# Spreading a transform stage over the opening of a training-step kernel, folding its edges in with the rest, and moving small sums off two borders

## The chip, the cores and the metric

The kernel runs on one core of a Trainium2 chip. The metric is the device time of that core in microseconds (us). The kernel before took 1378.1 us, the median of three runs from 1374.69 to 1380.41.

## The reference, cut to what matters

The program computes a layer forward and, from `grad_out`, all its gradients. Sequence length S is 2048, width D is 1024, hidden width F is 3584, all tensors are bf16.

```python
g = sigmoid((x * gate_w).sum(-1, keepdims=True))
a = irfft2(rfft2(x) * (w_r + 1j * w_i))            # a filter over the whole S x D plane
h = relu(x @ w1 + b1) ** 2
b = h @ w2 + b2
out = g * a + (1 - g) * b
# outputs: out, and the gradients of x, w_r, w_i, w1, b1, w2, b2, gate_w
```

Two of the small outputs are sums over columns: the gradient of `b2` (`out_7` in the kernel) and that of `gate_w` (`out_8`). The gradient of `b1` is `out_5`.

## The kernel before

The kernel has four stretches in time:

- the opening (to about 97 us): transposes of x and of the gradient, the gate, the first pair of hidden blocks, and the first stage of the two-dimensional transform for the 16 tiles of x;
- pass 1 (to about 480 us): the products `ph` = x·w1 and `pd` = gradient·w2ᵀ for each hidden block, with the first transform stage of the gradient's 16 tiles mixed in;
- pass 2: the gradients of the weights (`pw`), with the middle and the last transform stages mixed in;
- the last products (`acc`, `accg`), which give `out` and the gradient of x.

One tile of the first stage goes through five steps. VectorE (DVE) folds the tile by sums and differences, TensorE (PE) does eight small products into `pk`, ScalarE (ACT) copies them to `ft`, PE does eight more into `pu`, ACT copies them to `u`, and a store issued from GpSimd (POOL) sends `u` to memory.

```python
def folds(fb, xt, earlier=None):
    uv = fb.tile([P, 2, H], FDT, name="uv", tag="uv", bufs=2)
    after(V(out=uv[:, 0, :], in0=xt[:, 0:H], in1=xt[:, H:D], op=ALU.add), earlier, mybir.DependencyClass.NoSync)
    V(out=uv[:, 1, :], in0=xt[:, 0:H], in1=xt[:, H:D], op=ALU.subtract)
    ...
    V(out=f[:, 4, 0:1], in0=uv[:, 0, 0:1], in1=uv[:, 0, Q : Q + 1], op=ALU.add)
    V(out=f[:, 4, P : P + 1], in0=uv[:, 0, 0:1], in1=uv[:, 0, Q : Q + 1], op=ALU.subtract)

def one_s1(fb, cf, T, i, f, kmat, earlier=None):
    ...                                            # pk, then ft by ACT
    pu = fps.tile([P, 2, H], FP32, name="pu", tag="ps2", bufs=2)
    column_stage(FWD, pu, ft, cf)                  # reads ft at once
    u = fb.tile([P, D], FDT, name="u", tag="u", bufs=2)
    ...                                            # u by ACT, then st(out=z_scr..., in_=u)
```

`after(ins, earlier, NoSync)` only fixes an order: in the compiled program `ins` stands behind `earlier`. `st` issues a transfer from POOL, `ld` one from SyncE (SP). In the driver the x tiles come in bunches of four; the gradient's follow at a quarter of a step for each step of the main work, from -1.5:

```python
for i0 in range(0, NT, 4):
    ...                                            # gate, turns, transposes, next(units)
    for i in range(i0, i0 + 4):
        one_s1(f1, cf, 0, i, folds(f1, xs[i]), kf[:])
first = first_stage_of_grad()
mixed = spread(units, first, 0.25, -1.5)
```

`move()` loads the turned w2 blocks (`w2T`) of the next group from memory by SP, and `group()` loads the first operand of pass 2 (`grp`) by SP as well.

## Time and profile before

| | before |
|---|---|
| span of the profiled execution | 1374.2 us |
| PE busy | 1339.7 us (97%) |
| end of the opening (80 to 94 us) | PE 10.27 of 14 us, clock 0.87 |
| end of the last PE instruction to the end of the span | 7.9 us |

PE bounds the kernel, so every gain must come out of the 34.5 us in which PE is idle, out of time at a lowered clock, or out of the end. The lines for this are in the prediction below.

### The profile page before, as it was taken

How to read it: one execution, taken by the hardware profiler on the slowest of the kernel's cores; microseconds unless marked ns; L12 is line 12 of the kernel's file. 1: busy time of each engine (PE TensorE's matmuls, PEld its weight loads, DVE VectorE, ACT ScalarE, POOL GpSimd, SP SyncE). 2: the span in 40 equal slices, each digit the busy share in tenths (PEclk: the TensorE clock that was granted, in tenths of full speed). 3: DMA queues.
4: the chain of work that ended last, by engine and by line, in shares of the span. 5: the costliest groups of instructions: out<-in, count | busy, mean ns of one | idle time of the engine just before them, and what ended most of it. 6: DMA issues, size and time to landing. Idle time of an engine off the chain costs nothing.

```text
span 1374.2 us, 18936 instructions
## 1 busy us (share of the span) xinstructions
PE 1339.7 (97%) x7146; PEld 643.0 (47%) x7146; DVE 750.9 (55%) x1541; ACT 409.7 (30%) x626; POOL 291.3 (21%) x469
## 2 busy tenths in 40 slices
PE   7989999999999999999999999999999999999997
PEld 5644444444444444444444444555545444444443
DVE  6966666666665575564445643323856575642222
ACT  6753344444443312222323223433212100000000
POOL 0222222322232233433432212212001000000000
PEclk9999999999999999999999999999999999999999
DMA  7547777787779778789677458766898664653430
GB/s 272 188 169 210 250 230 237 240 250 240 218 240 266 222 234 191 206 211 216 184 184 196 99 151 245 234 228 206 249 230 231 177 199 130 200 159 103 135 100 23
DMA packets 217029, 273.32 MB, mean 199 GB/s; under 512 B 16988, under 2 KB 152170, under 8 KB 216938
## 3 DMA queue, kind: packets, MB, share of 16 engines
q1 hardware_dynamic: 181162, 153.58, 41.8%
q0 software_dynamic: 35776, 118.54, 26.7%
q8 instruction: 56, 0.92, 0.3%
q14 instruction: 35, 0.29, 0.1%
HBM read 147.25 MB, written 118.51 MB: 193 GB/s over the span
## 4 chain that ended last, share of the span: by engine, by line
PE 50%; issue 37%; POOL 4%; DMA 2%; DVE 2%; ACT 1%; SPq 1%; POOLq 0%; DVEq 0%; ACTq 0%
PE pw L783 14%; PE pd L593 12%; PE ph L583 11%; PE pw L800 7%; PE pu L278 1%; DMA w1g<-in_B_w_dram 1%; POOL ax_scr L490 1%; POOL out_dram L809 1%; POOL out_dram L914 1%; POOL out_dram L873 1%; PE pk L251 1%; PE pv L363 1%; DMA z_scr<-u 1%; PE px L318 1%; PE px L317 1%
## 5 line engine op out<-in xcount | busy, mean ns | idle before, releaser
L583 PE MATMUL ph<-xT,w1g 128*128 128x512 bf16 x896 | 221.2, 384 | 1.2 <-ACT rT L585 1.2
L593 PE MATMUL pd<-dbT,w2T 128*128 128x512 bf16 x896 | 212.6, 380 | 5.2 <-issue 1.8
L800 PE MATMUL pw<-grd,res 128*128 128x512 bf16 x896 | 200.2, 379 | 0.0
L783 PE MATMUL pw<-dbn,grp 128*128 128x512 bf16 x896 | 198.0, 379 | 1.6 <-DVE row L735 1.6
L866 PE MATMUL acc<-w,hblk 128*128 128x512 bf16 x896 | 198.1, 379 | 1.2 <-DVE bGo L868 1.2
L907 PE MATMUL accg<-w1Tr,hblk 128*128 128x512 bf16 x896 | 193.6, 379 | 0.0
L593 PEld LDWEIGHTS <-w2T 128*128 128x128 bf16 x896 | 87.3, 98 | 110.5 <-issue 6.2
L907 PEld LDWEIGHTS <-hblk 128*128 128x128 bf16 x896 | 87.7, 98 | 105.7
L783 PEld LDWEIGHTS <-grp 128*128 128x128 bf16 x896 | 87.0, 98 | 105.9 <-issue 2.5
L583 PEld LDWEIGHTS <-w1g 128*128 128x128 bf16 x896 | 87.3, 99 | 100.8 <-issue 6.7
L866 PEld LDWEIGHTS <-hblk 128*128 128x128 bf16 x896 | 87.0, 98 | 100.8 <-issue 1.5
L800 PEld LDWEIGHTS <-res 128*128 128x128 bf16 x896 | 86.6, 98 | 98.8
L585 ACT ACTIVATE rT<-ph,b1col 128x512 bf16<-128x512 f32 x112 | 77.2, 689 | 180.4 <-PE ph L583 180.3
L597 DVE SCALAR_TENSOR_TENSOR dhT<-pd,rT 128x512 bf16<-128x512 f32 x112 | 75.4, 673 | 82.4 <-PE pd L593 65.9
L787 ACT CAST wo<-pw 128x512 bf16<-128x512 f32 x56 | 32.8, 586 | 164.9 <-PE pw L783 158.9
L912 DVE TENSOR_TENSOR gxo<-accg,g 128x512 bf16<-128x512 f32 x32 | 22.1, 691 | 107.4 <-PE accg L907 107.2
L698 DVE STREAM_TRANSPOSE stg<-h2T 128x512 int32<-128x512 int32 x56 | 39.6, 708 | 71.7 <-ACT h2T L586 71.7
L319 DVE CAST x<-px 128x1024 f16<-128x1024 f32 x16 | 19.6, 1225 | 107.2 <-PE px L318 107.2
L795 POOL DMA_DIRECT2D out_dram<-wo x112 | 56.2, 515 | 84.1 <-ACT wo L787 78.3
L805 ACT CAST wo<-pw 128x512 bf16<-128x512 f32 x56 | 32.9, 587 | 132.0 <-PE pw L800 125.7
L586 ACT ACTIVATE h2T<-rT 128x512 bf16<-128x512 bf16 x112 | 70.8, 632 | 3.0
L705 DVE STREAM_TRANSPOSE stgd<-dhT 128x1024 bf16<-128x1024 bf16 x56 | 68.7, 1228 | 0.7
(177 smaller groups left out, 1431.2 us busy)
## 6 DMA issues: line engine op xcount, KB each, us to landing
h2T_scr<-h2T POOLq DMA_DIRECT2D x28, 512.0 KB, 5.3
h_scr<-stg POOLq DMA_DIRECT2D x28, 512.0 KB, 6.9
dhT_scr<-dhT POOLq DMA_DIRECT2D x28, 512.0 KB, 7.1
dh_scr<-stgd POOLq DMA_DIRECT2D x28, 512.0 KB, 6.8
grp<-h_scr SPq DMA_DIRECT2D x112, 128.0 KB
grd<-dh_scr SPq DMA_DIRECT2D x112, 128.0 KB
hblk<-h2T_scr SPq DMA_DIRECT2D x8, 1792.0 KB
hblk<-dhT_scr SPq DMA_DIRECT2D x8, 1792.0 KB
```

Source lines behind the costliest of these rows:

```text
L583: mm(ph[:], lhsT=w1g[:, dc, fc % 2 * P : (fc % 2 + 1) * P], rhs=xT[:, dc, ss], start=(dc == 0), stop=(dc == DC - 1))
L585: nc.scalar.activation(rT[:], ph[:], ACT.Relu, bias=b1col[:, fc : fc + 1])
L586: nc.scalar.activation(h2T, rT[:], ACT.Square)
L593: mm(pd[:], lhsT=w_[:, ec // 2, ec % 2 :: 2], rhs=dbT[:, ec, ss], start=(ec == 0), stop=(ec == DC - 1),)
L597: return STT(out=dhT, in0=pd[:], scalar=2.0, in1=rT[:], op0=ALU.mult, op1=ALU.mult, accum_out=gb1part[:, fc, sb : sb + 1],)
L698: nc.vector.transpose(out=stg[:, :, c, :], in_=h2T[:, c, :].bitcast(I32).rearrange("p (b i) -> p b i", i=32))
L705: nc.vector.transpose(out=stg[:, :, :, c, :].rearrange("p b k i -> p k b i"), in_=dhT[:, c, :].rearrange("p (k b i) -> p k b i", b=4, i=32),)
L783: mm(pw[:], lhsT=cur[:, t // 2, 2 * fb_ * P + t % 2 : 2 * (fb_ + 1) * P : 2], rhs=dbn[:, t, hf * H : (hf + 1) * H], start=(t == 0), stop=( ...
L795: st(out=dst[q], in_=wo[32 * q : 32 * (q + 1), :])
L800: mm(pw[:], lhsT=xr[t][:, d_ * P : (d_ + 1) * P], rhs=cur[:, t], start=(t == 0), stop=(t == NT - 1),)
L866: mm(acc[:], lhsT=cur[:, fc, t2::2], rhs=w2[:, fc, cs], start=(fc == 0), stop=(fc == FC - 1))
L907: mm(acc[:], lhsT=cur[:, fc, t2::2], rhs=w1T[:, fc, 2 * hf : 2 * hf + 2, :], start=(fc == 0), stop=(fc == FC - 1),)
```

## The change

The intent has four parts. The first stage of x becomes a generator of half steps (rows, then columns of the tile before) that the driver pulls between the other parts of the opening, and the second pair of w2 turns comes earlier. The gradient's first stage is cut into the same half steps and runs at 0.55 of a step for each step of the main work, so it ends earlier. The edges of the folds are folded with the rest: two DVE operations on single elements go. The small sums leave the border between the passes, and the last column sum goes ahead of the last half product; the last store of the gradient of x is issued from SP.

```diff
-        V(out=uv[:, 1, :], in0=xt[:, 0:H], in1=xt[:, H:D], op=ALU.subtract)
+        after(V(out=uv[:, 1, :], in0=xt[:, 0:H], in1=xt[:, H:D], op=ALU.subtract), earlier, mybir.DependencyClass.NoSync)
...
-        nc.scalar.copy(out=f[:, 3, 0:1], in_=uv[:, 1, 0:1])
-        nc.scalar.copy(out=f[:, 1, 0:1], in_=uv[:, 1, Q : Q + 1])
-        b0, b1 = f[:, 0:3:2, 1:P], f[:, 0:3:2, Q - 1 : P : -1]
-        V(out=f[:, 4:6, 1:P], in0=b0, in1=b1, op=ALU.add)
-        V(out=f[:, 4:6, P + 1 : Q], in0=b0, in1=b1, op=ALU.subtract)
-        V(out=f[:, 4, 0:1], ..., op=ALU.add)
-        V(out=f[:, 4, P : P + 1], ..., op=ALU.subtract)
+        nc.scalar.copy(out=f[:, 3:0:-2, 0], in_=uv[:, 1, 0 : Q + 1 : Q])
+        nc.scalar.copy(out=f[:, 0:3:2, 0 : Q + 1 : Q], in_=uv[:, 0:1, 0 : Q + 1 : Q].to_broadcast([P, 2, 2]))
+        b0, b1 = f[:, 0:3:2, 0:P], f[:, 0:3:2, Q:P:-1]
+        V(out=f[:, 4:6, 0:P], in0=b0, in1=b1, op=ALU.add)
+        V(out=f[:, 4:6, P:Q], in0=b0, in1=b1, op=ALU.subtract)
...
+    def first_stage_of_x():
+        ft = {}
+        for i in range(NT + 1):
+            if i < NT:
+                ft[i] = row_stage(f1, folds(f1, xs[i]), kf[:])
+                yield
+            if i > 0:
+                first_columns(f1, cf, 0, i - 1, ft[i - 1])
+                yield
...                                # first_stage_of_grad: rows, yield, columns, yield
-            if fg == 0:
-                turns = [turn_w2(2 * fp), turn_w2(2 * fp + 1)]
+            if fp == 0:
+                turns = [turn_w2(0), turn_w2(1)]
+                    if fp == 0 and sb == 1:
+                        turns = [turn_w2(2), turn_w2(3)]
...                                # the block for gb1 moves from the end of pass 1 to n == 1 of pass 2
-                column_sums(wb, mps, "pw", acc, out_7)
+                column_sums(wb, tps, "tr", acc, out_7)
...
+                    if t == NT - 1 and hf == 1:
+                        column_sums(wb, mps, "acc", gacc, out_8, 4)
-                st(out=o1_perm[t], in_=ot[:])
-        column_sums(wb, mps, "acc", gacc, out_8, 4)
+                (st if t < NT - 1 else ld)(out=o1_perm[t], in_=ot[:])
...                                # driver: next(stage, None) at eight places of each round
-    mixed = spread(units, first, 0.25, -1.5)
+    mixed = spread(units, first, 0.55)
```

More of the change, by code (lines that the diff above doesn't have):

```diff
@@ L231, in folds @@
         after(V(out=uv[:, 0, :], in0=xt[:, 0:H], in1=xt[:, H:D], op=ALU.add), earlier, mybir.DependencyClass.NoSync)
-        V(out=uv[:, 1, :], in0=xt[:, 0:H], in1=xt[:, H:D], op=ALU.subtract)
-        f = fb.tile([P, 6, Q], FDT, name="f", tag="f", bufs=2)
+        after(V(out=uv[:, 1, :], in0=xt[:, 0:H], in1=xt[:, H:D], op=ALU.subtract), earlier, mybir.DependencyClass.NoSync)
+        f = fb.tile([P, 6, Q + 2], FDT, name="f", tag="f", bufs=2)
         a0, a1 = uv[:, :, 1:Q], uv[:, :, H - 1 : Q : -1]
@@ L237, in folds, with row_stage @@
         V(out=f[:, 2:4, 1:Q], in0=a0, in1=a1, op=ALU.subtract)
-        nc.scalar.copy(out=f[:, 3, 0:1], in_=uv[:, 1, 0:1])
-        nc.scalar.copy(out=f[:, 1, 0:1], in_=uv[:, 1, Q : Q + 1])
-        b0, b1 = f[:, 0:3:2, 1:P], f[:, 0:3:2, Q - 1 : P : -1]
-        V(out=f[:, 4:6, 1:P], in0=b0, in1=b1, op=ALU.add)
-        V(out=f[:, 4:6, P + 1 : Q], in0=b0, in1=b1, op=ALU.subtract)
-        V(out=f[:, 4, 0:1], in0=uv[:, 0, 0:1], in1=uv[:, 0, Q : Q + 1], op=ALU.add)
-        V(out=f[:, 4, P : P + 1], in0=uv[:, 0, 0:1], in1=uv[:, 0, Q : Q + 1], op=ALU.subtract)
+        nc.scalar.copy(out=f[:, 3:0:-2, 0], in_=uv[:, 1, 0 : Q + 1 : Q])
[3 more added lines that the diff above has]
+        V(out=f[:, 4:6, P:Q], in0=b0, in1=b1, op=ALU.subtract)
         nc.scalar.copy(out=f[:, 5, P::-P], in_=f[:, 0:3:2, P])
         return f
-    def one_s1(fb, cf, T, i, f, kmat, earlier=None):
+    def row_stage(fb, f, kmat, earlier=None):
         pk = fps.tile([P, 8, P], FP32, name="pk", tag="ps2", bufs=2)
@@ L255, in one_s1, with first_columns @@
         nc.scalar.copy(out=ft[:], in_=pk[:])
+        return ft
+    def first_columns(fb, cf, T, i, ft, earlier=None):
         pu = fps.tile([P, 2, H], FP32, name="pu", tag="ps2", bufs=2)
-        column_stage(FWD, pu, ft, cf)
+        column_stage(FWD, pu, ft, cf, earlier)
         u = fb.tile([P, D], FDT, name="u", tag="u", bufs=2)
@@ L270, with column_stage @@
     INV = FWD[:4] + ((1, 0, Q, 0, 1), (1, 0, Q, 0, 2), (1, Q, Q, 0, 1), (1, Q, Q, 0, 2))
-    def column_stage(table, pu, ft, mat):
+    def column_stage(table, pu, ft, mat, earlier=None):
         o = 0
@@ L277, in column_stage @@
                 out = pu[:, bank, :].rearrange("p (h c i) -> p c h i", h=2, c=2)[:, lo // P]
-            mm(
+            first_ = mm(
                 out, lhsT=ft[:, b, :], rhs=mat[:, o : o + n],
@@ L281, in column_stage @@
             )
+            if o == 0:
+                after(first_, earlier, mybir.DependencyClass.NoSync)
             o += n
@@ L552, in gate @@
             nc.vector.tensor_scalar(out=dbn[:, i, :], in0=dbn[:, i, :], scalar1=omg[:, i : i + 1], scalar2=None, op0=ALU.mult)
+    def first_stage_of_x():
[7 more added lines that the diff above has]
+                yield
     def first_stage_of_grad():
-        f, kg = {}, {}
+        f, kg, ft = {}, {}, {}
         for n in range(NT + 4):
@@ L560, in first_stage_of_grad @@
             if i >= 0:
-                one_s1(f1, cf, 1, i, f[i], kg[i][:], later["last"])
+                ft[i] = row_stage(f1, f[i], kg[i][:], later["last"])
             i = n - 3
@@ L566, in first_stage_of_grad @@
                 f[i] = folds(f1, xs[i], later["last"])
+            yield
+            i = n - 4
+            if i >= 0:
+                first_columns(f1, cf, 1, i, ft[i], later["last"])
             yield
@@ L713, in mlp_in @@
                 st(out=dhT_scr[2 * fp : 2 * fp + 2, :, cols2].rearrange("c p s -> p c s"), in_=dhT[:])
-        gb1 = wb.tile([P, FC], FP32, name="gb1", tag="gb1")
-        nc.vector.reduce_sum(out=gb1[:], in_=gb1part[:], axis=mybir.AxisListType.X)
-        gb1b = wb.tile([P, FC], BF16, name="gb1b", tag="gb1b")
-        nc.vector.tensor_copy(out=gb1b[:], in_=gb1[:])
-        pb1 = tps.tile([FC, P], BF16, name="pb1", tag="tr", bufs=2)
-        nc.tensor.transpose(pb1[:], gb1b[:], identb[:])
-        gb1r = wb.tile([FC, P], BF16, name="gb1r", tag="gb1r")
-        nc.vector.tensor_copy(out=gb1r[:], in_=pb1[:])
-        st(out=out_5.rearrange("(fc p) -> fc p", p=P), in_=gb1r[:])
         mpss.close()
@@ L775, in mlp_grads @@
             if n == 1:
-                column_sums(wb, mps, "pw", acc, out_7)
+                column_sums(wb, tps, "tr", acc, out_7)
+                gb1 = wb.tile([P, FC], FP32, name="gb1", tag="gb1")
+                nc.vector.reduce_sum(out=gb1[:], in_=gb1part[:], axis=mybir.AxisListType.X)
+                gb1b = wb.tile([P, FC], BF16, name="gb1b", tag="gb1b")
+                nc.vector.tensor_copy(out=gb1b[:], in_=gb1[:])
+                pb1 = tps.tile([FC, P], BF16, name="pb1", tag="tr", bufs=2)
+                nc.tensor.transpose(pb1[:], gb1b[:], identb[:])
+                gb1r = wb.tile([FC, P], BF16, name="gb1r", tag="gb1r")
+                nc.vector.tensor_copy(out=gb1r[:], in_=pb1[:])
+                st(out=out_5.rearrange("(fc p) -> fc p", p=P), in_=gb1r[:])
             if scr is h2_scr:
@@ L903, in mlp_out @@
                 for hf in range(NH):
-                    cs = slice(hf * H, (hf + 1) * H)
+                    if t == NT - 1 and hf == 1:
+                        column_sums(wb, mps, "acc", gacc, out_8, 4)
                     acc = mps.tile([P, H], FP32, name="accg", tag="acc", bufs=4)
@@ L941 @@
     vectors(vrow)
+    stage = first_stage_of_x()
     for i0 in range(0, NT, 4):
@@ L948 @@
         gate(i0)
+        next(stage, None)
         next(units)
+        next(stage, None)
         for k in (i0 // 2, i0 // 2 + 1):
             turned(dbT, k, lambda i: dbn[:, i, :], of_tile, nc.vector.tensor_copy)
+            next(stage, None)
         if i0 + 4 < NT:
-            x_pair(i0 // 2 + 2), x_pair(i0 // 2 + 3)
+            for k in (i0 // 2 + 2, i0 // 2 + 3):
+                x_pair(k)
+                next(stage, None)
         next(units)
-        for i in range(i0, i0 + 4):
-            one_s1(f1, cf, 0, i, folds(f1, xs[i]), kf[:])
+        next(stage, None)
+        next(stage, None)
+    for _ in stage:
+        pass
     V(out=gpg[:], in0=gcol[:], in1=omg[:], op=ALU.mult)
```

## The prediction

> **What bounds the kernel now.** I read the page first: how busy each engine is, and in which slices. Then the table of windows, to find where TensorE (PE) isn't busy or runs at a lowered clock; then the timeline and the chain of waits at those places; last the instructions of the end.
>
> ```profile
> PE 1339.7 (97%) x7146; PEld 643.0 (47%) x7146; DVE 750.9 (55%) x1541; ACT 409.7 (30%) x626; POOL 291.3 (21%) x469
> ...
> PEclk9999999999999999999999999999999999999999
> ```
>
> PE is busy in 1339.7 of 1374.2 us, so only 34.5 us is idle. The change removes no matrix product, so it can win only what lies in those 34.5 us, in time at a lowered clock, and in the end. 2% would be 27.6 us of the 1378.1 us median. Summing the windows, the idle time splits so: 13.9 us in the first 100 us (4.1 of it the first load, which nothing here touches), 1.2 us at 124, 1.6 us in small pieces to 400 us, 3.0 us at 424 to 430, 2.8 us at the border of two passes, 3.8 us in the later stages, and 7.9 us after the last PE instruction. Columns of the next view: window, its length, busy us and instructions of PE, weight load, DVE, ACT, POOL, then PE clock, DMA share, GB/s.
>
> ```profile
> 40.00:80.00 40.00, 38.31 (x418) 26.37 (x415) 39.09 (x101) 30.43 (x64) 8.63 (x14) 1.00 0.50 172
> 80.00:94.00 14.00, 10.27 (x85) 6.34 (x84) 8.62 (x18) 8.24 (x12) 4.27 (x6) 0.87 0.58 196
> 94.00:360.00 266.00, 262.85 (x1333) 123.65 (x1332) 168.83 (x359) 119.04 (x207) 70.78 (x90) 0.99 0.75 233
> ```
>
> From 40 to 80 us PE and DVE are both nearly full. The hole is at 80 to 94, the end of the opening, where the last tiles of x's first stage stand one behind the other. The timeline there:
>
> ```profile
> 87.49 1.25 PE L593 MATMUL pd<-dbT,w2T 128*128 128x512 bf16 x5 [0.62 <-DVE w2T L615]
> 91.33 1.57 PE L278 MATMUL pu<-cf,ft 128*128 128x256 f16 x8 [2.59 <-ACT ft L255]
> ...
> 93.98 3.46 PE L583 MATMUL ph<-xT,w1g 128*128 128x512 bf16 x8
> ...
> 89.35 1.01 ACT L260 CAST u<-pu 128x1024 f16<-128x1024 f32 x1 [2.63 <-DMA z_scr<-u]
> ```
>
> PE waits 2.59 us for ft, ACT makes ft only after an earlier copy into u, and that copy waits for a store of u to land (the chain of waits has that store at 82.15 for 7.12 us). There are two u buffers, so tiles that come faster than one per half a landing stall. Eight products then take 3.46 us where later groups show 1.89: the windows show a granted clock of 0.50 from 91 to 97 us.
>
> The other two places, the pass border and the end:
>
> ```profile
> 484.91 0.23 PE L720 MATMUL pb<-identb,gb1b 128*28 128x128 bf16 x1 [1.16 <-DVE gb1b L718]
> ...
> 516.80 10.52 PE L783 MATMUL pw<-dbn,grp 128*128 128x512 bf16 x48 [1.61 <-DVE row L735]
> ```
>
> ```profile
> 1364.47 1.88 PE L734 MATMUL prow<-gacc,ones_f 128*1 128x512 f32 x4
> ...
> 1366.38 0.68 DVE L735 CAST row<-prow 1x512 bf16<-1x512 f32 x1 [0.18 <-PE prow L734]
> 1367.35 0.53 POOL L736 DMA_DIRECT2D out_dram<-row  x1 [1.25 <-DVE row L735]
> ```
>
> ```profile
> L1013 POOLq DRAIN  x3: 40/102/6101, 1367.3 to 1373.9; - x3
> ```
>
> At 484.91 PE waits in order for a small transpose of the bias sums; at 516.80 it waits because the column sums sit in the product's own two accumulators. After the last product (it ends near 1364.5) come the column sum, its copy, its store from POOL, and then a drain of POOL's queue of 6.1 us from 1367.3 to 1373.4. The store itself lands about 1.6 us after its issue by the list of issues, near 1369, so the drain, not the data, sets the end.
>
> **What the Trainium skill says.** "TensorE: Matmul & The Clock Gate", section "What's actually happening": an idle window of about 3.4 us puts PE at half clock, and about as long a busy stretch restores it. The trace agrees on the factor (0.50), with a gap of 2.59 us after smaller ones and a slow stretch of some 6.5 us. "DMA: Bandwidth & Descriptors", section "Anatomy of one DMA — SWDGE (gpsimd) path": most of a transfer's fixed cost of about 2 us is the receipt of the write. The trace agrees where the queues are empty (2.4 us for 256 KB at the end), not in the opening (7.12). "VectorE: DVE Perf Modes", section "The TRN2 errata": each operation on SBUF pays a fixed time. Here a fold of one element takes 155 ns, one of 254 elements 284 ns. The same page, "The DRAIN you can't avoid", puts the boilerplate drains at about 12 ns; this trace has one of 6101 ns.
>
> **The change part by part.**
>
> *Spreading x's first stage.* It removes the bunching: some 32 half steps (rows, then columns of the tile before) over about 80 us are one tile per 5 us, over 3.5 us, half of the 7.1 us landing. Lost in 80 to 97 us now: gaps of 0.25, 0.28, 0.62 and 2.59, together 3.7 us, and the half clock over 5.7 busy us (91 to 97), which is 2.8 us; 6.5 us in all. The 0.62 is the second pair of w2 turns, now moved earlier. I count 5.5 us as recovered, since the last tile still drains at the end.
>
> *Folds.* Two DVE operations of 155 ns go; in the timeline they start 70 ns apart, so 0.14 us of DVE per tile, 2.2 us for x's 16 tiles and as much for the gradient's. PE hardly waits on DVE, so I count 0.5 us. ACT keeps three small copies per tile. Against it: the second folds now read an edge that ACT copies, so DVE, in order, can stand behind ACT, itself often behind PE (ACT waits for ph 180.3 us in total). Where the compiled order is off by a microsecond, DVE stands. I charge 1.0 us in the opening. Opening: 5.5 + 0.5 - 1.0 = 5.0 us.
>
> *The gradient's first stage* in 40 half steps at 0.55 per unit of the main work: 73 of the 78 units, against 20 steps at 0.25 from -1.5, which left two for afterwards. PE's idle there is only 1.2 us (a late load at 124) and 1.6 us (four waits of 0.4 for dhT and crumbs). I gain 0.8 and charge 0.8 for DVE behind ACT: 0.
>
> *Pass border.* The waits of 1.16 and 1.61, 2.8 us, go; the matrix work stays. The small sums now use the transposes' buffers, which the spectra use too; I leave 0.6 for a new wait. Gain 2.2 us.
>
> *End.* The column sum's 1.88 us of PE moves ahead of the last half product, which ends at 1364.5 + 1.9 = 1366.4. The addition takes 0.69, signal about 0.3: issue at 1367.4. A load of 256 KB from SP in an idle machine took from its issue at 1.13 to its use at 4.11, 3.0 us; a POOL store 2.4. With 2.7 as an estimate it lands at 1370.1, and the closing semaphores, 0.8 us (1373.4 to 1374.2), give 1370.9. POOL's last issue comes a half product (6.05 us) earlier, so its drain ends near 1367.4, hidden. Gain 3.3; I take 3.0, for a store from SP stands nowhere in this trace.
>
> Sum: 5.0 + 0 + 2.2 + 3.0 = 10.2 us. 1378.1 - 10.2 = 1367.9.
>
> **The rivals.** (a) *DVE becomes the bound of the opening.* For it: 39.09 of 40 us busy, and 2.45 us of w2 turns move into that stretch, about what the folds save. Against: PE has only 1.7 us of idle there. It would take the opening's gain to about 1 us: 1372. (b) *The new wait of DVE on ACT spreads.* Over 32 tiles a stall of 0.4 us each is 13 us of DVE; a third reaching PE is 4 us: also 1372, with both 1376. (c) *The tail gains nothing*, if the drain of POOL follows the end of the program and not its own last store: then the end lies 6 us after 1370, some 1376, and the tail loses 2 us: 1373. The drain's start right at the last POOL issue speaks against it. (d) *Everything lines up*: the opening's other crumbs (4.6 us between 20 and 80) shrink too and the pace of the gradient's tiles removes the idle at 124: 1361.
>
> **Range and chances.** Three runs of before spread over 5.7 us, so a median carries some 2 us. Rivals a to c pull up by 4 to 5 each, d down by 7: 1361 to 1375. No stage holds the 27.6 us that 2% needs, and nothing adds work for PE: faster 0.02, within 2% 0.96, slower 0.02.
>
> **What would show it.** Right: no PE wait over 1 us between 80 and 97 us, granted clock 1.0 there, the first stage of x done some 5 us earlier; no wait on gb1b or row near 480 to 520; the last store on SP, the 6.1 us drain beginning before the last product's end, and under 5 us from that end to the span's. Wrong: DVE idle ahead of the second folds for an ACT copy, a half-clock stretch elsewhere in the opening, or the drain still last.

## The result, and the profile after

The changed kernel took 1363.49 us, the median of four runs from 1360.13 to 1363.86, against 1376.39 us for the kernel before in four runs. (With the fourth run the median of the kernel before is 1.7 us lower than the 1378.1 us that the prediction starts from.) The ratio is 0.99, with a 95% interval of 0.9866 to 0.9934. A ratio here is the mean time of one kernel's runs over that of the other's of the same rounds, so it is not quite the ratio of the medians that are quoted. The gain of the medians is 12.9 us; 10.2 were predicted. The profiled spans are 1374.2 and 1361.4 us.

The page after, busy time by engine and PE's granted clock in 40 slices:

```profile
PE 1328.8 (98%) x7036; PEld 644.0 (47%) x7146; DVE 750.1 (55%) x1477; ACT 415.1 (30%) x626; POOL 292.8 (22%) x468
...
PEclk9999999999998999999999999999999999999999
```

Two things are to be seen. The trace after lacks 110 records of products (7036, against 7146 weight loads), so PE's busy sums of the two pages can't be set against each other. And one slice now has a lower clock, at 408 to 442 us, where before had none.

**An account that does not use PE's busy time.** Each weight load stands for one product, and both traces have all 7146. I count each at what its columns take back to back (512 columns take 0.216 us in both traces: eight follow in 1.72 us) and add these up to any point. Time minus that work is time lost so far. Compared at equal work, the two traces give this table. The places are times in the trace before; the figures are worked out, and good to some tenths of a us.

| stretch | lost before | lost after | gained | predicted |
|---|---|---|---|---|
| to 79 us | 19.0 | 18.7 | 0.4 | } 5.0 |
| end of the opening, 79 to 102 | 7.4 | 2.1 | 5.3 | } |
| gradient's stage, 102 to 414 | 7.5 | 1.45 | 6.0 | 0 |
| late w2 blocks, 414 to 457 | 3.3 | 7.6 | -4.3 | 0 |
| border and column sums, 457 to 520 | 3.2 | 0.35 | 2.9 | 2.2 |
| the later stages | 11.2 | 12.5 | -1.3 | 0 |
| the end | | | 3.8 | 3.0 |
| sum | | | 12.8 | 10.2 |

A landmark that needs no account agrees: ACT's last `rT` of pass 1 starts at 479.04 us before and at 471.66 us after, 7.4 us earlier; the account has 0.4 + 5.3 + 6.0 - 4.3 = 7.4.

**The opening.** The windows of the page before and after for the same 20 us (window, length, busy us and instructions of PE, PEld, DVE, ACT, POOL, then PE clock, DMA share, GB/s), first of the kernel before:

```profile
80.00:100.00 20.00, 16.27 (x105) 8.77 (x104) 10.01 (x22) 9.61 (x14) 4.83 (x7) 0.83 0.51 179
```

The same window of the changed kernel, and from its timeline (start, length, instruction, in brackets the idle time before it and what ended it) the largest wait of PE that is left there:

```profile
80.00:100.00 20.00, 18.39 (x108) 9.40 (x109) 9.52 (x21) 10.57 (x17) 4.27 (x6) 1.00 0.54 181
```

```profile
93.35 1.89 PE L602 MATMUL ph<-xT,w1g 128*128 128x512 bf16 x8 [1.50 <-ACT rT L604]
```

The clock is 1.00 instead of 0.83, and the waits of 2.59 us for `ft` and 0.62 us for `w2T` are gone. On the side of the weight loads, the waits for `ft` up to 102 us fall from 9.0 us in 14 to 0.5 in one; but a new kind appears, 3.1 us in seven, for the edges of `f` that ACT copies (more of it at e10_folds_old_held). What is left at the end is again the drain of the last tiles: ACT stands for 3.8 us at a copy into `u` until the store of an earlier `u` has landed, and the `rT` behind it comes late.

**The gradient's stage.** The waits of the kernel before from 100 to 380 us (what waited, for what; us in total, times, longest):

```profile
PEld L278 <- ACT ft L255: 7.2, 14, 0.5
...
PE pd L593 <- DVE dhT L597: 1.6, 4, 0.4
...
PE ph L583 <- ACT rT L585: 1.2, 1, 1.2
```

The same view of the changed kernel, all that waits on PE's side:

```profile
PEld L612 <- issue: 1.2, 2, 1.0
PE pd L612 <- DVE dhT L616: 0.9, 2, 0.7
```

Fourteen waits for `ft` before, none after. The prediction missed them because it read PE alone. The timeline of the kernel before shows why that hides them:

```profile
205.94 0.62 PEld L278 LDWEIGHTS <-ft 128*128 128x128 f16 x8 [0.52 <-ACT ft L255]
205.94 0.91 PE L278 MATMUL pu<-cf,ft 128*128 128x256 f16 x8
```

The weight load of the column step stands 0.52 us for `ft`, and the product it belongs to starts at the same moment. But the PE line shows no idle time before it, as the products ahead are drawn longer than they run: the five of `ph` just before stand there for 1.24 us from 204.67, and five at 0.216 us are 1.08. The Trainium skill, page "Perfetto Trace Analysis", section "Tensor Engine Instruction (MATMUL, LD_WEIGHTS)", says that the end of a TensorE record is estimated and not observed. This trace agrees: 14 weight-load waits of 0.5 us left no mark on the PE lines, and the account puts some 0.3 us of lost time on each (an estimate: the stretch's gain without the waits that PE's own line shows, shared among fourteen). With a half step of main work between rows and columns, `ft` is always there.

**The late w2 blocks.** This is where the change gives time back. The timeline of the changed kernel:

```profile
416.46 3.15 PE L612 MATMUL pd<-dbT,w2T 128*128 128x512 bf16 x7 [4.23 <-DMA w2T<-stg]
...
423.11 1.89 PE L612 MATMUL pd<-dbT,w2T 128*128 128x512 bf16 x8 [0.70 <-DMA w2T<-stg]
```

PE waits 4.23 us, and the seven products after the wait take 3.15 us: half clock. SP's own timeline says why the blocks come late, first in the kernel before, then in the changed one:

```profile
393.34 24.27 SPq L759 DMA_DIRECT2D grp<-h_scr  x12
417.71 7.78 SPq L641 DMA_DIRECT2D w2T<-stg  x8
```

```profile
388.56 20.81 SPq L770 DMA_DIRECT2D grp<-h_scr  x12
409.47 12.83 SPq L660 DMA_DIRECT2D w2T<-stg  x12
```

SP issues its loads in one order. The twelve loads of `grp` for pass 2 are not urgent, but they stand ahead of loads of `w2T` that PE needs at once, and they take 21 to 24 us to issue. From 342 us to the first of these `w2T` loads, SP had issued twelve loads of `grp` in the kernel before and 25 in the changed one (12 at 360.31, one at 381.53, and the 12 shown). The faster stage frees the buffers that `grp` goes into sooner, and the compiled order of SP's loads moved with it. In the kernel before this already cost 3.3 us; now it costs 7.6.

**The end.** The timeline of the changed kernel, and the summary of POOL's drains (count, then shortest, middle and longest in ns, then when the first and the last start):

```profile
1349.42 1.88 PE L745 MATMUL prow<-gacc,ones_f 128*1 128x512 f32 x4
...
1351.23 6.22 PE L929 MATMUL accg<-w1Tr,hblk 128*128 128x512 bf16 x27
...
1357.48 0.69 DVE L934 TENSOR_TENSOR gxo<-accg,g 128x512 bf16<-128x512 f32 x1 [5.47 <-PE accg L929]
1358.20 0.34 SPq L936 DMA_DIRECT2D out_dram<-gxo  x1
```

```profile
L1042 POOLq DRAIN  x3: 40/102/6267, 1352.3 to 1361.1; - x3
```

The three drains of that line are POOL's, at different times; the long one is the one that counts. The column sum stands ahead of the last half product. POOL's last issue is now the small row at 1352.30, its drain of 6.27 us begins there, before the product ends at 1357.45, and is out of the way. From the product's end to the end of the span there are 3.92 us; before, from 1364.54, there were 9.66, of which 1.88 was the sum.

### The profile page after: what moved, and what is told of

It reads as the page before. It is cut to its first block, busy times and chain, and to the rows that moved or that the text cites. A ratio compares the mean times of both kernels' runs of the same rounds, so it can differ in the third digit from the quotient of the medians.

```text
span 1361.4 us, 18729 instructions
## 1 busy us (share of the span) xinstructions
PE 1328.8 (98%) x7036; PEld 644.0 (47%) x7146; DVE 750.1 (55%) x1477; ACT 415.1 (30%) x626; POOL 292.8 (22%) x468
## 5 line engine op out<-in xcount | busy, mean ns | idle before, releaser
L602 PE MATMUL ph<-xT,w1g 128*128 128x512 bf16 x866 | 214.8, 382 | 4.3 <-ACT rT L604 1.5
```

What stands on the lines that cost most here:

```text
L602: mm(ph[:], lhsT=w1g[:, dc, fc % 2 * P : (fc % 2 + 1) * P], rhs=xT[:, dc, ss], start=(dc == 0), stop=(dc == DC - 1))
```

## The experiments

The theory: the end gains by POOL's drain starting early; the gradient's stage gains by `ft` being ready; the stall at 416 us is the order of SP's queue; the opening gains by the spread. The rivals: the end gains by moving the sums; the gradient's gain is noise or comes from the new folds; the stall is memory traffic. The first four kernels ran in one batch (the kernel before there: median 1375.87 of 11 runs), each one edit away from the changed kernel, which itself ran in an earlier batch (before: 1376.39). Between batches I compare medians, and give the difference by the ratios beside it where it is another; the two differ by up to 2 us, as the kernel before itself spreads over 7 to 10 us within a batch.

**The last store back on POOL (e1_tail_pool).**

```diff
-                (st if t < NT - 1 else ld)(out=o1_perm[t], in_=ot[:])
+                st(out=o1_perm[t], in_=ot[:])
```

> The changed kernel with one edit: the last store of the second output goes out from GpSimd again, not from SP; the column sums stay ahead of the last product. My theory: the span's end is set by the drain of GpSimd's queue, 6.1 us from its last issue. The drain would then start at about 1358.4 instead of 1352, so the span ends some 0.7 + 0.3 + 6.1 + 0.8 us after the last product: near 1365.4, 4 us longer than the changed kernel's 1361.4; the profile shows a drain of about 6 us that begins after the last product. Rival: the end is set by the store's own landing, and a store of 256 KB lands in 2.4 us from GpSimd and as fast from SP: then this run is within 0.5 us of the changed kernel, and all of the tail's gain came from moving the sums.

Measured: 1366.6 us (1366.02 to 1367.72), ratio 0.9932: 3.1 us slower than the changed kernel by the medians, 4.4 by the ratios, 3.8 by the profiled spans, where 4 were expected. Its timeline and the drain:

```profile
1358.06 0.56 POOL L936 DMA_DIRECT2D out_dram<-gxo  x1 [5.65 <-DVE gxo L934]
```

```profile
L1042 POOLq DRAIN  x3: 40/93/6381, 1358.0 to 1364.9; - x3
```

The drain starts with the store and takes 6.38 us again. From the product's end to the span's end it is 8.15 us instead of 3.92, although the data landed 2.3 us after the issue. With the sums ahead but the store on POOL, 1.88 + 8.15 = 10.0 us would stand where before had 9.66: moving the sums alone gains nothing.

**The gradient's stage as before (e2_grad_unsplit).**

```diff
                 ft[i] = row_stage(f1, f[i], kg[i][:], later["last"])
+                first_columns(f1, cf, 1, i, ft[i], later["last"])
...
-            i = n - 4
-            if i >= 0:
-                first_columns(f1, cf, 1, i, ft[i], later["last"])
-            yield
...
-    mixed = spread(units, first, 0.55)
+    mixed = spread(units, first, 0.25, -1.5)
```

> The changed kernel with the gradient's first stage as before: rows and columns of a tile in one step, 0.25 steps per unit of the main work from -1.5. My theory from the two traces: two effects of opposite sign sit in this part. The weight loads of the column stage wait for ft again (7.2 us in 14 waits from 100 to 380 us before, some 0.3 us of TensorE each), and dhT waits of 0.4 to 0.6 us come back: +6 us. The first stage ends later, so the loads of the next pass's groups no longer hold up the last w2T moves so long: -4.3 us. Net +1.7 us: about 1365.2 where the changed kernel has 1363.5. Rival: the 6 us come from the opening's new order or from the shorter folds and not from the split; then the waits for ft stay away and only the -4.3 shows: about 1359.

Measured: 1365.18 us (1360.79 to 1369.46), ratio 0.9924. The runs spread over 8.7 us, so the trace has to decide. Its waits from 100 to 380 us:

```profile
PEld L280 <- ACT ft L254: 7.2, 14, 0.5
```

The fourteen waits are back to the digit, with the new folds in place, so the folds are not their cure. By the account this stretch loses 7.0 us (1.45 in the changed kernel), and the late w2 blocks cost 3.5 us (7.6). The two parts nearly cancel, which is why this part of the change as a whole is worth little: 1.7 us by the medians, 3.3 by the ratios, 1.4 by the profiled spans.

**The split at the old pace (e3_split_old_pace).** Half steps, but twice as many at the old rate, so that the stage ends when it used to.

```diff
-    mixed = spread(units, first, 0.55)
+    mixed = spread(units, first, 0.5, -3.0)
```

> The changed kernel with the split into half steps kept and the pace of before: 0.5 half steps per unit from -3.0, the same tiles at the same units as before. My theory: the split removes the waits for ft whatever the pace, and the stall of 4.23 us on w2T near 412 us comes of the faster pace, which frees the first stage's buffers earlier, so that 12 more loads of the next pass's groups stand ahead of the w2T moves in SP's queue. So the stall falls back to the two waits of 1.2 and 1.8 us of before: -4.3 us, about 1359. Rival: the stall comes of the transfers' total load at that time, not of the queue's order; then nothing changes: 1363.5.

Measured: 1357.82 us (1356.58 to 1361.75), ratio 0.9872; 5.7 us faster than the changed kernel by the medians, 3.9 by the ratios. The waits for `ft` are 1.0 us in two, so the split is worth its gain without the faster pace. SP's order goes back with the pace, to that of e2_grad_unsplit:

```profile
382.19 22.18 SPq L770 DMA_DIRECT2D grp<-h_scr  x11
404.47 10.58 SPq L660 DMA_DIRECT2D w2T<-stg  x8
```

Eleven loads of `grp` stand ahead of these `w2T` now, not 25. But the profiled run was the slowest of the six. It still shows waits of 1.48 and 2.93 us for `w2T`, 4.4 in all against 4.9 in the changed kernel, and by the account the late blocks cost 6.3 us (7.6). The pace moves the order, that is shown; that the stall falls with it, as was expected, is not shown by this trace, and the faster runs were not traced.

**The loads of `grp` held behind those of `w2T` (e4_grp_held).**

```diff
-                    ld(out=t_[32 * b : 32 * (b + 1)], in_=v_[32 * a : 32 * (a + 1), :, b, :])
+                    later["moved"] = ld(out=t_[32 * b : 32 * (b + 1)], in_=v_[32 * a : 32 * (a + 1), :, b, :])
...
-                    ld(out=t_[32 * b : 32 * (b + 1), :, a, :], in_=v_[a, b])
+                    after(
+                        ld(out=t_[32 * b : 32 * (b + 1), :, a, :], in_=v_[a, b]),
+                        later["moved"], mybir.DependencyClass.NoSync,
+                    )
```

> The changed kernel with one order added on SP's queue: the loads of the next pass's groups (grp) come after the last moves of w2T. My theory: the weight loads near 412 us find w2T in place, the idle 4.23, 0.22 and 0.70 us and the half-clock stretch after them go, together 7.6 us of TensorE; the groups' loads then take some 45 us of issuing from 405 us, and the first has landed before the pass border near 470. About 1356.5. Rival: the first group or z now comes late, and TensorE waits at the pass border for what it no longer waits for at 412: 1360 to 1364.

Measured: 1354.61 us (1353.91 to 1355.09), ratio 0.9844 with an interval of 0.9821 to 0.9867. SP's timeline:

```profile
399.68 10.49 SPq L660 DMA_DIRECT2D w2T<-stg  x11
...
417.12 2.97 SPq L771 DMA_DIRECT2D grp<-h_scr  x2
```

The w2 loads go first, PE has no wait from 405 to 432 us, and none for `grp` at the border. An order on SP alone, with no transfer removed, wins 8.9 us over the changed kernel by the medians and 7.7 by the ratios; by the account the late blocks cost 7.6 us in the changed kernel and nothing here. The rival (memory traffic) falls. This version beats both kernels; the rest of the experiments start from it. The next four ran in a second batch (before: 1374.60) and the last four in a third (before: 1378.21).

**x in bunches again, the w2 turns left early (e5_x_bunched).**

```diff
-        next(stage, None)                          # and the other seven places
...
-            for k in (i0 // 2 + 2, i0 // 2 + 3):
-                x_pair(k)
-                next(stage, None)
+            x_pair(i0 // 2 + 2), x_pair(i0 // 2 + 3)
...
+        for i in range(i0, i0 + 4):
+            first_columns(f1, cf, 0, i, row_stage(f1, folds(f1, xs[i]), kf[:]))
```

> The kernel with the groups' loads held back (e4, 1354.6 us), with x's first stage bunched again: the four tiles of a quarter one behind the other, as before, all else kept (w2 turns early, shorter folds). My theory: the last tiles stand behind two u buffers, so a gap of about 2.6 us and the half clock after it come back between 80 and 97 us: up by 5 us to about 1359.6. Rival: what won the 5.7 us in the opening was the earlier w2 turns and the shorter folds on a full DVE, and the tiles' order is of no account: then at most 1 us is lost, 1355.5.

Measured: 1356.34 us (1354.49 to 1356.98), ratio 0.9862: 1.7 us slower than e4_grp_held, 2.5 by the ratios, 2.8 by the account. This missed the expectation. PE's largest waits for `ft` at the end of the opening are 0.28 and 0.76 us, the clock stays at 1.00. With the turns early, PE has products of pass 1 to put between the bunched tiles.

**Sums after the last product, both last stores from SP (e6_sums_late_sp).**

```diff
-    def column_sums(sb_pool, ps_pool, tag, acc, dst, bufs=2):
+    def column_sums(sb_pool, ps_pool, tag, acc, dst, bufs=2, put=st):
...
-        st(out=dst.rearrange("(o d) -> o d", o=1), in_=row[:])
+        put(out=dst.rearrange("(o d) -> o d", o=1), in_=row[:])
...
-                    if t == NT - 1 and hf == 1:
-                        column_sums(wb, mps, "acc", gacc, out_8, 4)
...
+        column_sums(wb, mps, "acc", gacc, out_8, 4, ld)
```

> The kernel e4 (1354.6 us) with the column sums after the last product again, but with both last stores from SP. My theory: what counts at the end is that nothing is issued from GpSimd late. The sums' 1.9 us of TensorE stand on the path in either place: product end + 1.9 for the sums, 0.7 for the copy, 0.3 + 2.0 for the small store and 0.8 for the closing is 5.7 us, against 1.9 + 3.9 = 5.8 now. So the same within 0.7 us: 1354 to 1355.3, and no drain at the end. Rival: putting the sums ahead is worth their 1.9 us by itself: 1356.5.

Measured: 1353.82 us (1353.28 to 1354.49), ratio 0.9846. The end of its timeline:

```profile
1347.69 0.34 SPq L937 DMA_DIRECT2D out_dram<-gxo  x1
...
1349.49 0.27 SPq L747 DMA_DIRECT2D out_dram<-row  x1
```

The span ends at 1351.7. The sums run beside the landing of the large store, and it matters little where they stand (this end is some 0.7 us shorter by the account). With e1_tail_pool this settles the end: what counts is that POOL issues nothing late.

**The folds of before, whole (e7_folds_old).** The edit puts back the old `folds`, and with it the second fold without its tie.

```diff
-        after(V(out=uv[:, 1, :], ..., op=ALU.subtract), earlier, mybir.DependencyClass.NoSync)
+        V(out=uv[:, 1, :], ..., op=ALU.subtract)
...                                # and the edges of f as in the kernel before
```

> The kernel e4 (1354.6 us) with the folds of before: edges by two more DVE operations of 155 ns per tile. My theory: DVE carries 2.2 us more in the opening and as much in the gradient's stage, of which TensorE feels some 0.5 us: 1355.1, the same within noise. Rival a (DVE bounds the opening): up by 2 us and more, and more idle of TensorE between 20 and 90 us. Rival b (the new wait of DVE on ACT's edge copies costs): down by 1 us or more.

Measured: 1364.16 us (1363.75 to 1367.21), ratio 0.9926: 9.6 us slower than e4_grp_held, 11.3 by the ratios, against an expected 0.5. I had mixed two edits. PE waited 11.09 us near 102 us for a `dhT` that stood on DVE behind a fold, whose source had not landed; the next batch took the two apart.

**The border as before (e8_border_old).** The block for `gb1` back to the end of pass 1, the column sums back in the accumulators `pw`.

```diff
-                column_sums(wb, tps, "tr", acc, out_7)
+                column_sums(wb, mps, "pw", acc, out_7)
...                                # and the nine lines from gb1 = ... to st(out=out_5...) before mpss.close()
```

> The kernel e4 (1354.6 us) with the small sums where they were: the bias sums at the end of the first pass, the column sums in the product's own accumulators. My theory: the waits of 1.16 us on gb1b at the border and of 1.61 us on row come back, and with what the modelled matmul ends hide, 2.9 us: 1357.5. Rival: the other changes have moved DVE's work so that it is free at these two places, and nothing comes back: 1354.6.

Measured: 1358.22 us (1356.19 to 1360.24), ratio 0.9876: 3.6 us slower than e4_grp_held, 4.4 by the ratios. Its timeline:

```profile
470.03 0.23 PE L740 MATMUL pb<-identb,gb1b 128*28 128x128 bf16 x1 [1.16 <-DVE gb1b L738]
...
501.93 10.52 PE L807 MATMUL pw<-dbn,grp 128*128 128x512 bf16 x47 [1.61 <-DVE row L755]
```

Both waits of before are back, of the same size to the hundredth. By the account the first costs 1.44 and the second about 1.9 us, 3.3 in all, 2.9 more than the changed kernel loses in this stretch.

**A third u buffer (e9_three_u).** To make room for the third `u`, one of the eight `src` went.

```diff
-        u = fb.tile([P, D], FDT, name="u", tag="u", bufs=2)
+        u = fb.tile([P, D], FDT, name="u", tag="u", bufs=3)
...
-        src = f1.tile([P, D], BF16, name="src", tag="src", bufs=8)
+        src = f1.tile([P, D], BF16, name="src", tag="src", bufs=7)
```

> The kernel e4 (1354.6 us) with three buffers for u and, to make room, seven instead of eight for the sources. My theory: in e4 TensorE still waits 1.53 us at 92.8 us because ACT stands 3.86 us before a copy into u until a store of u has landed, the same cause as the 2.59 us of before. With a third buffer that wait goes: 1353. Rival: the store's landing is only the last of several things that ACT's queue waits for there, or the missing source costs as much: 1354.6 or more.

Measured: 1355.89 us (1355.03 to 1356.41), ratio 0.984: no gain, where 1353 was expected. ACT's wait for the store of `u` and PE's wait near 93 us are gone, but a new one stands at 104 us:

```profile
104.69 3.30 PE L612 MATMUL pd<-dbT,w2T 128*128 128x512 bf16 x8 [2.30 <-DVE dhT L616]
```

DVE was waiting 2.08 us for a load of w2 (`w2r`). The mechanism was right and the gain was not: by the account the run is 2.7 us ahead of e4_grp_held at the end of the opening, and PE runs on into the next late transfer. The missing `src` is not the cause of that stall: e10_folds_old_held has eight, and there PE waits 2.25 us at the same place, also behind a `w2r` that is 2.1 us late.

**The old folds with both first folds tied (e10_folds_old_held).**

```diff
         after(V(out=uv[:, 1, :], ..., op=ALU.subtract), earlier, mybir.DependencyClass.NoSync)   # kept
...                                # the edges of f as in the kernel before
```

> The kernel e4 with the folds of before, but with both first folds of a tile tied behind the paced instruction, as the change has it. My theory after e7: the 9.6 us there came of the missing tie of the second fold alone (it stood early in DVE's queue and waited 14.4 us for its source), not of the two more operations; so this run is near e4, 1354.6 to 1355.6, and no DVE wait of over 3 us for a source of the gradient. Rival: the folds' own time or the copies of the edges do it: 1358 or more.

Measured: 1353.4 us (1352.89 to 1354.48), ratio 0.9821. By medians this is 1.2 us faster than e4_grp_held, by ratios 3.2; in any case it is no slower. The shorter folds are worth nothing here, and the loss of e7_folds_old was not theirs. The waits of the weight loads over the whole span, first of e4_grp_held, then of this kernel, show what the new folds cost:

```profile
PEld L250 <- ACT f L244: 3.2, 7, 0.7
```

```profile
PEld L251 <- ACT f L245: 0.5, 1, 0.5
```

With the new folds and spread tiles the row step waits for ACT's edge copies seven times; with the old ones, once. By the account this kernel has lost 2.5 us less than e4_grp_held by the end of the opening, and it gives that back at the late `w2r` near 104 us. So in the opening the new folds did harm, which the total hides. How much of the 2.5 us is due to these seven waits was not tested.

**The new folds without that tie (e11_no_hold).**

```diff
-        after(V(out=uv[:, 1, :], ..., op=ALU.subtract), earlier, mybir.DependencyClass.NoSync)
+        V(out=uv[:, 1, :], ..., op=ALU.subtract)
```

> The kernel e4 with that tie alone taken away, the folds as short as in the change. My theory: the second fold stands early in DVE's order again (right behind the first dhT of the second pair of blocks), waits for its source while SP's queue is held by the w2r loads, and TensorE stalls some 11 us near 91 us with the half clock after it: 1363 to 1365. Rival: with the new folds DVE comes there later, the source has landed and little is lost: 1355 to 1357.

Measured: 1365.34 us (1364.68 to 1365.79), ratio 0.9908: 10.7 us slower than e4_grp_held, 8.8 by the ratios. The timeline:

```profile
102.59 0.42 DVE L232 TENSOR_TENSOR uv<-src 128x512 f16<-128x512 bf16 x1 [14.23 <-DMA src<-in_grad_out_dram]
...
103.68 3.57 PE L612 MATMUL pd<-dbT,w2T 128*128 128x512 bf16 x8 [9.33 <-DVE dhT L616]
```

One untied fold (L232 is the second one) was put ahead of pass 1's work in DVE's order. Its source was still on the way, so DVE stood 14.23 us and PE 9.33. A tie on a single instruction, which the diff shows in half a line, is worth more at this pace than the spreading of x and the early turns together (5.7 us by the account).

**The opening as before: x in bunches and the w2 turns late (e12_opening_old).** As e5_x_bunched, and besides:

```diff
-            if fp == 0:
-                turns = [turn_w2(0), turn_w2(1)]
+            if fg == 0:
+                turns = [turn_w2(2 * fp), turn_w2(2 * fp + 1)]
...
-                    if fp == 0 and sb == 1:
-                        turns = [turn_w2(2), turn_w2(3)]
```

> The kernel e4 with x's tiles bunched (as e5, 1356.3 us) and the second pair of w2 turns late, as before. My theory: the gap of 2.6 us with its half clock needs both, the bunched tiles and the turns that fall among the last of them; so this run loses what before lost in 80 to 97 us against the changed kernel, 5.7 us: 1360. Rival: the turns' place is worth only its 0.6 us of wait: 1357.

Measured: 1360.99 us (1360.19 to 1361.44), ratio 0.9877: 6.4 us slower than e4_grp_held, 4.5 by the ratios, 6.3 by the account. Its timeline:

```profile
88.51 0.82 PE L612 MATMUL pd<-dbT,w2T 128*128 128x512 bf16 x3 [1.57 <-DVE w2T L634]
...
93.34 1.01 ACT L262 CAST u<-pu 128x1024 f16<-128x1024 f32 x1 [4.24 <-DMA z_scr<-u]
...
95.32 0.91 PE L280 MATMUL pu<-cf,ft 128*128 128x256 f16 x8 [3.30 <-ACT ft L254]
```

The picture of the kernel before is back, longer by a little: PE for `ft`, ACT for the landing of `u`. The time lost by the end of the opening is 26.5 us, 26.4 in the kernel before. The clock stays at 1.00 this time. Bunches alone cost 1.7 to 2.8 us and late turns with them some 6: with the turns early, PE has something to do while the last tiles drain. The fourth case, spread tiles with late turns, was not run.

## Why the prediction was right or wrong

The predicted time and range were right: 1367.9 in 1361 to 1375, measured 1363.49, same within 2%. Of the 4.4 us between the two, 1.7 come from the lower median of the kernel before. That the gain came so near is in part luck: the sum hides two terms of the opposite sign, +6.0 and -4.3, that the prediction had as one zero.

**Opening: 5.0 predicted, 5.7 measured.** The cause was right: tiles faster than the landing of `u`. The parts were not. The 0.5 us for the folds is nothing, and in the opening rather a loss (e10_folds_old_held). The 1.0 us charged for DVE standing behind ACT showed as a single wait of 0.5 us; the charge itself was not idle, but what stood behind ACT's edge copies was PE's weight loads (3.1 us in seven waits). Bunches and late turns were counted as separate gaps of 2.59 and 0.62 us; e12_opening_old and e5_x_bunched show that they belong together, and that early turns alone remove over half of the loss (from 6.3 to 2.8 us by the account). The test for it, "no PE wait over 1 us between 80 and 97 us", failed by one wait of 1.50 us.

**Gradient's stage: 0 predicted, +6.0 and -4.3 measured.** This is the step that failed: "PE's idle there is only 1.2 us (a late load at 124) and 1.6 us (four waits of 0.4 for dhT and crumbs). I gain 0.8 and charge 0.8". The term is mis-sized because idle time was read from the PE lines alone. The weight loads' waits of 7.2 us were in the same trace, and e2_grad_unsplit brings them back. The second half of the error is that the faster pace had no consequence in the prediction: the buffers come free earlier, and SP's loads for pass 2 move ahead of those that pass 1 still needs. e4_grp_held removes exactly that, and e3_split_old_pace shows that the pace sets the order. The prediction also passed over the tie of the second fold. In the kernel before, which had no tie, DVE stood 2.29 us at that fold at 123 us for a late source and PE lost 1.2 us; at the new pace its lack costs 9 to 11 us (e11_no_hold).

**Border: 2.2 predicted, 2.9 measured.** The two waits went; the 0.6 us set aside for a new wait was not needed. e8_border_old puts them back for 3.6 us.

**End: 3.0 predicted, 3.8 measured.** The mechanism was right, and the store from SP landed about 2.0 us after its issue, where 2.7 was estimated. But the 1.88 us of the column sum, which the prediction carefully carried along, hardly matter (e6_sums_late_sp).

**The rivals.** (a), DVE as the bound: no wait of PE for DVE is left between 80 and 97 us, and two operations more per tile cost nothing (e10_folds_old_held), so it fell. (b), waits of DVE on ACT, fell in size: 2.2 us in seven waits over the whole span, where it had 13; the weight loads' waits for the same copies it did not name. (c), a drain tied to the end of the program, fell: it starts at POOL's last issue in both positions (e1_tail_pool). (d), everything lines up, came nearest: 1361 was its number, with a part of its reason, the idle at 124.

What stays open: why the later stages lose 1.3 us more by the account (one wait for a DVE result near 1090 us is 1.66 instead of 1.24, which is a third of it), and what of the batch differences of 1 to 3 us is the chip.

## What to carry to other kernels

Read the weight loads' waits as well as PE's: fourteen half-microsecond waits left PE "busy". When a change lets a side stage run sooner, follow what it frees: the loads that go into those buffers can move ahead of urgent ones in the same queue, and one tie of order then wins much (another 7.6 to 8.9 us here, beside the 12.9 of the whole change). Do not let the queue with the long closing drain issue the last store, and tie every instruction of a group that the scheduler can hoist, not only the first.

## What the Trainium skill lacked or had wrong

- "VectorE: DVE Perf Modes", section "The DRAIN you can't avoid", gives about 12 ns for the drains outside the kernel's own work. Here a drain of GpSimd's queue took 6.10, 6.27 and 6.38 us in three kernels, each time right from its last DMA issue; issued from SP, the last store has no such tail (3.92 instead of 8.15 us to the end). I found this in none of the pages I read.
- "TensorE: Matmul & The Clock Gate", section "What's actually happening", gives an idle window of about 3.4 us for half clock, and says that this window runs freely, whatever the kernel does. Here 2.59 us of idle (after smaller gaps) led to a clock of 0.50, while a gap of 3.30 us in e12_opening_old left the window from 80 to 100 us at 1.00. So the length of one gap doesn't decide it. A freely running window would allow that, but the section doesn't say how much work within a window still counts as idle, and no run here tests it.
- "Perfetto Trace Analysis", section "Tensor Engine Instruction (MATMUL, LD_WEIGHTS)", says that the end of a record is estimated, but not what it hides: a wait of 0.52 us at a weight load with no idle time on the PE line, 14 times, some 0.3 us of real time each.
- "DMA: Bandwidth & Descriptors", section "Anatomy of one DMA — SWDGE (gpsimd) path", gives a fixed cost of about 2 us for a transfer. A store of `u` in the loaded opening took 7.12 us from issue to landing, and twelve loads took 20.81 us only to be issued from SP, with urgent loads behind them (4.23 us of PE). I found no figure for such a stand in the queue there.
